# High part of x ahead of the sum in an FFT kernel's three-product mixing, inverse constants on SP's queue, two residues mixed plainly

## The chip, the cores and the metric

The kernel runs on one NeuronCore of a Trainium2 chip. Its engines are PE (TensorE, matmuls), DVE (VectorE), ACT (ScalarE), POOL (GpSimd) and SP (SyncE, which here only issues transfers). The metric is the device time of one execution in microseconds. A change is compared by the median of several runs of the kernel before and after it; smaller is better.

## What is computed

The reference is a chain of three layers on x of 4 x 3072 x 256 float32: a mixing layer in the frequency domain, a gated feed-forward layer and a channel-mix layer. Only the first is touched here.

```python
X = np.fft.rfft(x, axis=1)
Xr, Xi = X.real, X.imag
Yr = Xr @ w_r - Xi @ w_i + b_r
Yi = Xr @ w_i + Xi @ w_r + b_i
Yr = np.sign(Yr) * np.maximum(np.abs(Yr) - 0.01, 0.0)
Yi = np.sign(Yi) * np.maximum(np.abs(Yi) - 0.01, 0.0)
y = np.fft.irfft(Yr + 1j * Yi, n=3072, axis=1)
...                                    # feed-forward: h = y @ w_in; g = h * tanh(softplus(h)); x = g @ w_out
...                                    # channel mix: relu(xk @ w_k)**2 @ w_v, gated by sigmoid(xr @ w_r)
```

## The kernel before

**Two parts.** `part1` does the frequency layer, some 326 us of the span. `part2` does the other two layers; it is put in order by a planner of its own, and the diff doesn't touch it.

**Part 1 in steps.** A transform of 3072 points is split into 24 x 128. DVE does the 24-point butterflies on the batch's tile `a` (the "f1" operations, in the background), and PE does the 128-point transforms as matmuls with constants. The frequencies fall into NT = 12 residues per batch, and with 4 batches there are 48 residues u = 0 to 47. The loop at line 1011 makes one step per u. For a residue, the work is:

- F(u) (`emit_F`): 8 matmuls of `a` with forward constants `fm` into the PSUM tile `xps` (two banks in turn). The result holds the real part xr and the imaginary part xi.
- `post_F(u)`: its evacuation. Matmuls run on rounded "high" parts and on remainders, "low" parts, so `xh` is a copy of `xps` by ACT and `xl` is `xps` minus `xh` by DVE.
- Mixing, in one of two ways, into the PSUM tile `yps` (three banks in turn), which ACT fills with the bias first (`preload`). *Plain*: `emit_M`, 12 matmuls 512 wide, high x high, high x low and low x high. *Three-product* (`gauss(u)` true): G1 (`emit_G1`) multiplies the sum xr + xi by w_r into the first half of `yps`, ACT copies this half into the second (`copy_G`), and G2 (`emit_G2`) adds xr (w_i - w_r) and -xi (w_r + w_i). The sum needs an ACT copy of xr into `xsf`, a DVE addition of xi into `xsf`, and then a high and a low part of its own (the tile named `xs`).
- `post_M(u)`: the soft threshold, two ACT passes into `yb` (from u = 42 on one ACT pass and one of DVE).
- I(u) (`emit_I`): 8 matmuls of `yb` with the inverse constants `im` into `bps`. `post_I(u)` copies it with ACT to `bs`, and SP stores it.

In step u, instructions are emitted in this order: F of the residue ahead, `post_M(u-1)`, `post_I(u-2)`, `post_F` of the residue ahead, G1(u+1) and its copy, M(u) or G2(u), `preload(u+2)`, I(u-1), and the step's transfers. The residue ahead is u + 1 up to LEAD = 7 and u + 2 behind it; step 7 emits both F(8) and F(9). Each engine carries out its own instructions in that order. In steps 35 to 42 `post_I` stands later, behind the weights' work.

**Background work.** DVE also does the butterflies of the next batch, those of the inverse transform ("f3", tile `g`), and the preparation of weights for part 2. The class `Background` decides by a simple clock model where they are put between the steps' own DVE operations: `bg.until(t)` emits background operations until its model clock reaches t, `bg.spend(ready, cost)` charges the clock for the step's own work, and `bg.flush(due)` emits what must not come later. `pe` is the model's clock of PE, with T_F, T_M, T_G1, T_G2 and T_I as durations in ns, and `e` is the model's end of F.

**Queues.** The constants of I(u) come from DRAM, one load of 256 KB per residue, into three slots in turn. Load n may start when the inverse that last used its slot is done. It is emitted at the end of a step, right behind I(u-1), whose slot it takes, and it is needed by I(u+2). The first three go over SP's queue, the others over POOL's:

```python
(nc.gpsimd if n >= len(RING) else nc.sync).dma_start(out=z, in_=isrc[:, t])
```

POOL's queue also carries the loads of x that add to what is in the tile (`end_sum`, steps 6 and 17). SP's queue carries all other loads of x, the stores of `bs`, the loads of weights and the transfers of the inverse transform.

Of the kernel before, what the change touches and what calls it, by code (L numbers as in the profile page):

```python
# [11 lines left out]
F32 = mybir.dt.float32  # L12
F32R = mybir.dt.float32r
I32 = mybir.dt.int32
ACTF = mybir.ActivationFunctionType
ALU = mybir.AluOpType
ADD, SUB, MULT = ALU.add, ALU.subtract, ALU.mult
# [8 lines left out]
NB = 4  # L26
# [6 lines left out]
NT = 12  # L33
# [5 lines left out]
F1_AT = ((4, 4), (0, 0), (0, 0))  # L39
EARLY, REST, LAND = 4, 2, 3  # L40
START = (18600, 20500)
SLACK = (2000, 3200, 600, 1500)
T_F, T_M, T_G1, T_G2, T_I = 1600, 2860, 730, 1690, 1725

SUMS_AT = (11, 12, 23, 24)
# [4 lines left out]
LEAD = 7  # L50
# [131 lines left out]
def tile_fft_mix_moe_channel_mix(  # L182
# [19 lines left out]
    nc = tc.nc  # L202
# [3 lines left out]
    def pool(stack, name, bufs, **kw):  # L206
        return stack.enter_context(tc.tile_pool(name=name, bufs=bufs, reuse_waits="tile", **kw))
# [5 lines left out]
    def tt(o, a, b, op):  # L213
        V.tensor_tensor(out=o, in0=a, in1=b, op=op)  # L214
# [4 lines left out]
    def act(o, i, f, **kw):  # L219
        S.activation(out=o, in_=i, func=f, **kw)  # L220
# [16 lines left out]
    mat = pool(ctx, "mat", 1)  # L237
# [9 lines left out]
    RING = (14, 16, 17)  # L247
# [281 lines left out]
    bg = Background()  # L529
# [162 lines left out]
    def part1():  # L692
        with ExitStack() as es:
# [17 lines left out]
                load_x(As[b], b)  # L711

            xt, xsum, ybt, ybs, xps, yps, bps, lows, flow, xsp, spare = {}, {}, {}, {}, {}, {}, {}, {}, {}, {}, {}
            gauss = lambda u: u > LEAD + 1 and u % NT

            def emit_F(u):
                b, t = u // NT, ORD[u % NT]
                A = As[b]
                ps = psx.tile([128, 2, 256], F32, tag="x", name="xps")
                lr, li = LINES_F[t]  # L720
                line = lambda h, l: A[:, l, h, :]
                if b == 0 and t == 4:
                    lr, li = 20, 21
                if b == 0 and t < 4:
                    line = lambda h, l: G0[:, LINES_G[l - 16], h, :]
                half = lambda z, i: z.rearrange("p (r i f) -> p r i f", r=2, i=2)[:, :, i, :]
                for h in range(2):
                    if t:
                        mm(ps[:, h, :], line(h, lr), fm[t][:, 0, :], True, False)
                        mm(ps[:, h, :], line(h, li), fm[t][:, 1, :], False, True)  # L730
                    else:
                        for i, l in enumerate((lr, li)):
                            mm(half(ps[:, h, :], i), line(h, l), half(fm[0][:, i, :], i), True, True)
                xps[u] = ps
# [14 lines left out]
            def post_F(u):  # L749
                t = u % NT  # L750
                ps = xps.pop(u)
                if u % 3:
                    xh, xl = [xs_p.tile([128, 2, 256], F32R, tag=w, name=w) for w in ("xh", "xl")]
                else:
                    xh, xl = [slot(F32R, w, 2, i) for w, i in (("xh", 12), ("xl", 13))]
                if gauss(u):
                    act(xsf, ps[:, :, 0:128], ACTF.Copy)
                    tt(xsf, ps[:, :, 128:256], xsf, ADD)
                act(xh, ps, ACTF.Copy)
                tt(xl, ps, xh.bitcast(F32), SUB)  # L760
                xt[u] = (xh, xl)
                if gauss(u):
                    z = mat.tile([128, 512], F32R, tag="m%d" % (22 if u % 2 else 15), name="xs").rearrange(
                        "p (s h f) -> p s h f", s=2, h=2)
                    sh, sl = xsum[u] = z[:, 0], z[:, 1]
                    act(sh, xsf, ACTF.Copy)
                    tt(sl, xsf, sh.bitcast(F32), SUB)
                if t == 0:
                    zh, zl = (new_z(w).rearrange("p (h f) -> p h f", h=2) for w in ("zh", "zl"))
                    xt[u] += (zh, zl)  # L770
                    copy_z(u, 0)
                    if u == 0:
                        copy_z(u, 1)

            def copy_z(u, k):
                zz, xx = xt[u][2 + k], xt[u][k]
                S.activation(out=zz, in_=xx.bitcast(F32), func=ACTF.Copy)
                S.activation(out=zz.rearrange("p h (r f) -> p (h r) f", r=2)[:, :, 0:1],
                             in_=zero[:, 0:4].rearrange("p (a o) -> p a o", o=1), func=ACTF.Copy)

            def preload(u):
                ps = yps[u] = psy.tile([128, 512], F32, tag="y", name="yps")
                if gauss(u):
                    act(ps[:, 0:256], bias[:, 0:256], ACTF.Copy)
                    return
                act(ps, bias, ACTF.Copy)
                if u % NT == 0:
                    act(ps[0:1, 256:512], bias[0:1, 0:256], ACTF.Copy)
# [82 lines left out]
            def load_stream(n):  # L871
                _, u, kind = stream[n]
                t = ORD[u % NT]
                z = slot(F32 if kind == "im" else F32R, kind, 2, RING[n % len(RING)])
                (flow if kind == "fmlo" else lows if kind == "imlo" else im)[u] = z
                if kind == "im":
                    (nc.gpsimd if n >= len(RING) else nc.sync).dma_start(out=z, in_=isrc[:, t])
                else:
                    nc.gpsimd.dma_start(out=z, in_=planes[:, kind != "fmlo", t, kind != "imhi"].rearrange("p (r f) -> p r f", r=2))

# [37 lines left out]
            isrc = inv.rearrange("p t (r f) -> p t r f", r=2)  # L918
# [43 lines left out]
            m = split_mix(c1, mraw[0], 0) + split_mix(c1, mraw[1], 1)  # L962
            xsf = c1.tile([128, 2, 128], F32, name="xsf")
# [5 lines left out]
            def gauss_w(h):  # L969
                q = pools["st"].tile([128, 512], F32, tag="q", name="q", bufs=3)  # L970
                hi, lo = wt["gauss", h]
                wr, wi = mraw[h][:, 0, :], mraw[h][:, 1, :]

                def low():
                    act(hi, q, ACTF.Copy)
                    tt(lo, q, hi.bitcast(F32), SUB)
                return [(420.0, lambda: tt(q[:, 0:256], wi, wr, SUB)),
                        (420.0, lambda: stt(q[:, 256:512], wr, -1.0, wi, MULT, SUB)), (700.0, low)]

            def gauss_b():  # L980
                q = pools["st"].tile([128, 512], F32, tag="q", name="q", bufs=3)

                def low():
                    act(brow, q[:, 0:256], ACTF.Copy)
                    act(ones, fm[1][:, 0, 0:128], ACTF.Copy, scale=0.0, bias=1.0 / 64)
                    tt(brow[64:128], q[64:128, 0:256], brow[64:128].bitcast(F32), SUB)
                return [(420.0, lambda: tt(q[:, 0:256], bias[:, 256:512], bias[:, 0:256], SUB)), (420.0, low)]
# [8 lines left out]
            bg.add(priced(rest + first), 4)  # L996
            bg.add(priced(tail[:7]), 5)
            bg.add(priced(tail[7:]), 8)
            bg.add(gauss_w(0) + gauss_w(1) + gauss_b(), LEAD + 2)
            NU = NB * NT  # L1000
            mv[0] = ysrc = None

# [7 lines left out]
            x_at, y_at = {0: bg.clock}, 0.0  # L1010
            for u in range(NU):
                b, t = divmod(u, NT)
# [9 lines left out]
                if u == SUMS_AT[0] - 4:  # L1022
# [10 lines left out]
                                 [(group(g), 2, LOWS_AT - 2 + g, LOWS_AT + g) for g in range(4, 8)] +  # L1033
                                 [(lambda i=i: wout_piece(i), 2, LOWS_AT + 6 + k, LOWS_AT + 8 + k) for k, i in enumerate((0, 4, 1, 5))])
                    emit(wq.load(u))
                ahead = [v for v in ([u + 1] if u < LEAD else [u + 1, u + 2] if u == LEAD else [u + 2]) if v < NU]
                bg.flush(max(ahead, default=u))
                if u == 6:
                    S.activation(out=mu1, in_=mu, func=ACTF.Copy, scale=-1.0, bias=1.0)
                f_end = []  # L1040
# [8 lines left out]
                if u and u - 1 not in TWO_PASS:  # L1049
                    bg.until(y_at + (900 if u - 1 in SPLIT_I else SLACK[0]))  # L1050
                    post_M2(u - 1)
# [21 lines left out]
                behind = []  # L1073
                if u >= SUMS_AT[0] - 3:
                    emit(wq.sca(u, 2))
                    behind = wq.vec(u, 4)
                for v, e in zip(ahead, f_end):
                    bg.until(e + 700 + (0 if u == 0 else SLACK[2] if v % NT == 0 else SLACK[3] if gauss(v) else SLACK[1]) - sum(c for c, e in behind))
                    post_F(v)
                    x_at[v] = bg.spend(e + 700, 602)  # L1080
                    if gauss(v):
                        x_at[v] = bg.spend(e + 1300, 900)
                if u >= SUMS_AT[0] - 3:
                    bg.flush(-1)
                    for c, e in behind:
# [5 lines left out]
                if u + 1 < NU and gauss(u + 1):  # L1091
                    emit_G1(u + 1)
                    copy_G(u + 1)
                    pe = max(pe, x_at[u + 1] + 300) + T_G1
                emit_M(u, None if u else 1)
                if u + 2 < NU:
                    preload(u + 2)
                if (u + 1) % NT == 0 and u + 1 < NU:
                    copy_z(u + 1, 1)
                pe = pe + T_G2 if gauss(u) else max(pe, x_at[u] + 300) + (T_M if u else 900)  # L1100
                y_new = pe + 700
                if u:
                    emit_I(u - 1)
                    pe = max(pe, y_at + 300) + T_I
                y_at = y_new
                if u + NT in SPLIT_F:
                    load_fwd(u + NT)
# [569 lines left out]
```

## Time and profile before

| | us |
|---|---|
| median of 3 runs (1874.37 to 1876.4) | 1875.39 |
| the profiled execution, its own time | 1874.67 |
| its span, first to last instruction | 1872.9 |
| PE busy in the span | 1846.2 (99%) |
| DVE busy | 1413.5 (75%) |
| ACT busy | 1247.7 (67%) |
| POOL busy | 46.0 (2%) |

The span is what the profile shows; the rest of an execution's time lies around it. Times in rows count from the start of the span. A row of the timeline gives the start and the duration of an instruction, or of several merged ones, and in brackets how long its engine stood idle before it and what ended that idle time. Matmuls are pipelined: a row's duration holds the last one's way through the array as well, so the start of one group to the start of the next is the better measure of what a group costs.

### The profile page before, as it was taken

What the parts mean: (1) busy time and instruction counts of PE and PEld (TensorE: products, weight loads), DVE (VectorE), ACT (ScalarE), POOL (GpSimd) and SP (SyncE); (2) the same over time, 40 slices, a digit from 0 to 9 for tenths busy, and PEclk for the clock granted to TensorE, in tenths of its full rate; (3) what the DMA queues carried; (4) which work ended last, traced back from release to release, by engine and by line L of the source; (5) the groups of instructions that cost most, each with busy time, mean ns of one, the idle gap of its engine ahead of it and who ended that gap; (6) DMA issues with size and microseconds to landing.
All of it is one profiled execution on the core that took longest, in us unless ns stands there. A gap on an engine that the chain in (4) does not pass through costs nothing.

```text
span 1872.9 us, 27574 instructions
## 1 busy us (share of the span) xinstructions
PE 1846.2 (99%) x9902; PEld 1600.6 (85%) x9902; DVE 1413.5 (75%) x2537; ACT 1247.7 (67%) x2306; POOL 46.0 (2%) x74
## 2 busy tenths in 40 slices
PE   9899999999999999999999999999999999999999
PEld 7788887888888888888888888888999999999998
DVE  8888867888798879597877768576676666666654
ACT  3566588665667566575766657576877777777775
POOL 1211000000000000000000000000000000000000
PEclk9999999999999999999999999999999999999999
DMA  8849367645646554545546455452422222222211
GB/s 264 230 153 275 113 221 257 190 151 183 195 145 199 164 177 134 179 149 163 185 141 196 145 158 171 138 179 86 158 73 68 68 68 68 68 68 69 68 46 34
DMA packets 183016, 271.57 MB, mean 145 GB/s; under 512 B 16416, under 2 KB 106272, under 8 KB 182624
## 3 DMA queue, kind: packets, MB, share of 16 engines
q1 hardware_dynamic: 173920, 252.77, 42.9%
q0 software_dynamic: 7888, 15.99, 3.5%
q8 instruction: 79, 1.29, 0.3%
q10 hardware_dynamic: 1072, 1.05, 0.2%
q14 instruction: 57, 0.47, 0.1%
HBM read 193.20 MB, written 76.55 MB: 144 GB/s over the span
## 4 chain that ended last, share of the span: by engine, by line
PE 87%; DVE 5%; ACT 3%; DMA 3%; issue 1%; POOL 0%; SPq 0%; DVEq 0%; POOLq 0%; ACTq 0%
PE a L223 28%; PE x L223 16%; PE v L223 14%; PE c L223 10%; PE z L223 5%; PE d L223 5%; PE zps L223 4%; DMA a<-in_x_dram 2%; PE yps L223 2%; PE xps L223 1%; PE bps L223 1%; DVE a L214 1%; DMA im<-in_inv_dram 1%; ACT xh L220 1%; DVE g L214 1%
## 5 line engine op out<-in xcount | busy, mean ns | idle before, releaser
L214 DVE TENSOR_TENSOR l<-k,h 128x512 fp32r<-128x512 f32 x576 | 391.7, 688 | 304.7 <-ACT k L220 150.6
L223 PE MATMUL a<-h,wo 128*128 128x512 f32 x1536 | 520.8, 389 | 0.0
L223 PEld LDWEIGHTS a<-h,wo 128*128 128x128 f32 x1536 | 288.3, 188 | 60.1
L223 PE MATMUL a<-l,wo 128*128 128x512 f32 x768 | 298.8, 389 | 0.0
L223 PE MATMUL v<-wv,h 128*128 128x256 f32 x1536 | 274.4, 278 | 0.0
L223 PEld LDWEIGHTS v<-wv,h 128*128 128x128 f32 x1536 | 244.4, 188 | 13.7
L220 ACT ACTIVATE k<-c 128x512 f32<-128x512 f32 x288 | 172.9, 600 | 108.4 <-PE c L223 96.2
L223 PE MATMUL x<-yc,wr 128*128 128x512 f32 x864 | 243.2, 390 | 0.0
L220 ACT ACTIVATE c<-x 128x512 f32<-128x512 f32 x288 | 169.6, 589 | 89.4 <-PE x L223 75.0
L220 ACT ACTIVATE k<-k 128x512 f32<-128x512 f32 x288 | 178.1, 633 | 65.5 <-DVE k L214 63.3
L223 PE MATMUL v<-wv,l 128*128 128x256 f32 x768 | 213.0, 277 | 0.0
L223 PEld LDWEIGHTS x<-yc,wr 128*128 128x128 f32 x864 | 161.9, 188 | 34.5 <-ACT d L220 0.4
L220 ACT ACTIVATE d<-x 128x512 f32<-128x512 f32 x144 | 84.6, 587 | 145.7 <-PE x L223 144.6
L223 PEld LDWEIGHTS a<-l,wo 128*128 128x128 f32 x768 | 144.2, 188 | 29.9
L223 PE MATMUL c<-yc,wr 128*128 128x512 f32 x576 | 161.8, 389 | 0.0
L223 PEld LDWEIGHTS v<-wv,l 128*128 128x128 f32 x768 | 144.4, 188 | 0.0
L220 ACT ACTIVATE h<-k 128x512 fp32r<-128x512 f32 x192 | 118.6, 629 | 30.2 <-DVE k L217 28.2
L214 DVE TENSOR_TENSOR k<-d,zs 128x512 f32<-128x512 f32 x144 | 98.8, 686 | 42.4 <-PE d L223 42.0
L223 PEld LDWEIGHTS c<-yc,wr 128*128 128x128 f32 x576 | 108.1, 188 | 22.6
L214 DVE TENSOR_TENSOR yc<-src,yc 128x512 fp32r<-128x512 f32 x168 | 112.1, 686 | 14.3 <-ACT yc L220 13.8
L223 PE MATMUL x<-yc,wk 128*128 128x512 f32 x432 | 122.5, 392 | 0.0
L214 DVE TENSOR_TENSOR g<-g 128x128 f32<-128x128 f32 (+3 forms) x264 | 110.7, 442 | 0.9
(128 smaller groups left out, 2907.7 us busy)
## 6 DMA issues: line engine op xcount, KB each, us to landing
wr<-h_dr SPq DMA_DIRECT2D x288, 256.0 KB, 2.8
b_dr<-bs SPq DMA_DIRECT2D x48, 256.0 KB, 3.5
src<-y_dr SPq DMA_DIRECT2D x24, 512.0 KB, 4.1
wr<-h_dr SPq DMA_DIRECT2D x96, 128.0 KB, 2.1
xk_dr<-tm SPq DMA_DIRECT2D x48, 256.0 KB, 3.1
xr_dr<-tm SPq DMA_DIRECT2D x48, 256.0 KB, 3.2
xr<-xr_dr SPq DMA_DIRECT2D x24, 512.0 KB, 3.8
src<-xk_dr SPq DMA_DIRECT2D x24, 512.0 KB, 4.2
```

The costliest lines, as they stand in the source:

```text
L214: V.tensor_tensor(out=o, in0=a, in1=b, op=op)
L220: S.activation(out=o, in_=i, func=f, **kw)
L223: T.matmul(out=o, lhsT=l, rhs=r, start=start, stop=stop, **kw)
```

## The change

In three-product residues ACT now makes `xh` directly behind its copy of xr, and DVE's addition for the sum comes behind that. The sum's high and low part move out of `post_F` into a function `post_sum`, which is called at the end of the step, behind M(u) and `preload(u+2)`. The model's times for background work around them change with it. In step 7, F(9) and its evacuation move from behind F(8) to the end of the step. Residues 46 and 47 are mixed plainly. All inverse constants go over SP's queue. The weights of the three-product form get a later due time.

```diff
-SLACK = (2000, 3200, 600, 1500)
+SLACK = (2000, 3200, 600)
...
-            gauss = lambda u: u > LEAD + 1 and u % NT
+            gauss = lambda u: LEAD + 1 < u < NB * NT - 2 and u % NT
...
                 if gauss(u):
                     act(xsf, ps[:, :, 0:128], ACTF.Copy)
+                act(xh, ps, ACTF.Copy)
+                if gauss(u):
                     tt(xsf, ps[:, :, 128:256], xsf, ADD)
-                act(xh, ps, ACTF.Copy)
                 tt(xl, ps, xh.bitcast(F32), SUB)
                 xt[u] = (xh, xl)
-                if gauss(u):
-                    z = mat.tile([128, 512], F32R, tag="m%d" % (22 if u % 2 else 15), name="xs").rearrange(
-                        "p (s h f) -> p s h f", s=2, h=2)
-                    sh, sl = xsum[u] = z[:, 0], z[:, 1]
-                    act(sh, xsf, ACTF.Copy)
-                    tt(sl, xsf, sh.bitcast(F32), SUB)
...
+            def post_sum(u):
+                z = mat.tile([128, 512], F32R, tag="m%d" % (22 if u % 2 else 15), name="xs").rearrange(
+                    "p (s h f) -> p s h f", s=2, h=2)
+                sh, sl = xsum[u] = z[:, 0], z[:, 1]
+                act(sh, xsf, ACTF.Copy)
+                tt(sl, xsf, sh.bitcast(F32), SUB)
...
-                    (nc.gpsimd if n >= len(RING) else nc.sync).dma_start(out=z, in_=isrc[:, t])
+                    nc.sync.dma_start(out=z, in_=isrc[:, t])
...
-            bg.add(gauss_w(0) + gauss_w(1) + gauss_b(), LEAD + 2)
+            bg.add(gauss_w(0) + gauss_w(1) + gauss_b(), LEAD + 4)
...
-                ahead = [v for v in ([u + 1] if u < LEAD else [u + 1, u + 2] if u == LEAD else [u + 2]) if v < NU]
+                ahead = [v for v in [u + 1 if u <= LEAD else u + 2] if v < NU]
...
-                    bg.until(e + 700 + (0 if u == 0 else SLACK[2] if v % NT == 0 else SLACK[3] if gauss(v) else SLACK[1]) - sum(c for c, e in behind))
+                    bg.until(e + 1500 if gauss(v) else e + 700 + (0 if u == 0 else SLACK[2] if v % NT == 0 else SLACK[1]) - sum(c for c, e in behind))
                     post_F(v)
-                    x_at[v] = bg.spend(e + 700, 602)
-                    if gauss(v):
-                        x_at[v] = bg.spend(e + 1300, 900)
+                    x_at[v] = bg.spend(e + (1100 if gauss(v) else 700), 980 if gauss(v) else 602)
...
                 if u + 2 < NU:
                     preload(u + 2)
+                for v in ahead:
+                    if gauss(v):
+                        bg.until(f_end[0] + 2700)
+                        post_sum(v)
+                        x_at[v] = bg.spend(f_end[0] + 2700, 400)
...
                 if u:
                     emit_I(u - 1)
                     pe = max(pe, y_at + 300) + T_I
+                if u == LEAD:
+                    bg.flush(u + 2)
+                    emit_F(u + 2)
+                    pe += T_F
+                    bg.until(pe + 700)
+                    post_F(u + 2)
+                    post_sum(u + 2)
+                    x_at[u + 2] = bg.spend(pe + 1100, 1380)
```

## Rows read from the trace of the kernel before

**Rows 1.** Waits of PE, 15 to 330 us: total, times, longest

```profile
PE yps L223 <- ACT yps L220: 9.3, 13, 1.8
PE bps L223 <- DMA im<-in_inv_dram: 5.5, 2, 2.9
PE bps L223 <- DVE yb L217: 2.1, 3, 1.0
PE xps L223 <- DVE xl L214: 2.1, 2, 1.2
```

**Rows 2.** Timeline of PE: the inverse matmuls of steps 21 to 25

```profile
164.36 1.89 PE L223 MATMUL bps<-im,yb 128*128 128x256 f32 x8
169.25 1.89 PE L223 MATMUL bps<-im,yb 128*128 128x256 f32 x8
174.26 1.89 PE L223 MATMUL bps<-im,yb 128*128 128x256 f32 x8
181.30 1.89 PE L223 MATMUL bps<-im,yb 128*128 128x256 f32 x8
187.03 1.89 PE L223 MATMUL bps<-im,yb 128*128 128x256 f32 x8
```

**Rows 3.** Windows: busy PE, PEld, DVE, ACT, POOL, clock, DMA share, GB/s

```profile
103.56:181.30 77.74, 71.86 (x427) 64.41 (x426) 65.61 (x127) 46.12 (x105) 13.72 (x18) 0.98 0.82 234
181.30:257.88 76.58, 71.93 (x428) 64.64 (x427) 64.03 (x126) 44.69 (x104) 6.45 (x12) 0.98 0.40 122
257.88:311.52 53.64, 52.35 (x317) 47.44 (x316) 38.30 (x80) 48.44 (x106) 4.84 (x9) 1.00 0.88 297
```

**Rows 4.** Timeline of all engines around the longest wait of G1

```profile
239.91 0.42 DVE L214 TENSOR_TENSOR xsf<-xps,xsf 128x256 f32<-128x256 f32 x1
240.35 0.60 ACT L220 ACTIVATE xh<-xps 128x512 fp32r<-128x512 f32 x1 [3.75 <-DVE xsf L214]
...
241.46 0.37 ACT L220 ACTIVATE yps<-bias 128x256 f32<-128x256 f32 x1
...
241.88 0.50 PE L223 MATMUL yps<-wmh,xs 128*128 128x256 f32 x2 [1.84 <-ACT yps L220]
```

**Rows 5.** Waits of all engines, 15 to 330 us

```profile
ACT xh L220 <- DVE xsf L214: 70.6, 36, 5.3
...
DVE xl L214 <- ACT xh L220: 24.7, 38, 0.7
```

**Rows 6.** Timeline of POOL: three loads in one row

```profile
149.33 2.21 POOL L877 DMA_DIRECT2D im<-in_inv_dram  x3
```

**Rows 7.** Timeline of PE: inverses behind late constants, and the one between

```profile
84.90 2.57 PE L223 MATMUL bps<-im,yb 128*128 128x256 f32 x8 [2.62 <-DMA im<-in_inv_dram]
...
91.50 1.89 PE L223 MATMUL bps<-im,yb 128*128 128x256 f32 x8
...
156.88 2.85 PE L223 MATMUL bps<-im,yb 128*128 128x256 f32 x8 [2.88 <-DMA im<-in_inv_dram]
```

**Rows 8.** Window behind the first late constant, columns as in rows 3

```profile
85.00:89.00 4.00, 4.00 (x17) 3.60 (x18) 3.34 (x9) 3.10 (x7) 0.54 (x1) 0.64 1.09 376
```

**Rows 9.** DMA issues: size, median us to landing

```profile
im<-in_inv_dram POOLq DMA_DIRECT2D x45, 256.0 KB, 3.3
...
a<-in_x_dram SPq DMA_DIRECT2D x13, 512.0 KB, 9.0
```

**Rows 10.** Timeline of DVE and PE in step 8

```profile
70.36 0.68 DVE L214 TENSOR_TENSOR xl<-xps,xh 128x512 fp32r<-128x512 f32 x1
...
71.10 1.99 PE L223 MATMUL xps<-fm,a 128*128 128x256 f32 x8 [0.90 <-DVE xl L214]
```

**Rows 11.** Timeline of PE: two inverses with a plain step between

```profile
40.33 1.89 PE L223 MATMUL bps<-im,yb 128*128 128x256 f32 x8
...
46.52 1.89 PE L223 MATMUL bps<-im,yb 128*128 128x256 f32 x8
```

**Rows 12.** Tile `wg`, its making: ns least, median, most; first and last start

```profile
L214 DVE TENSOR_TENSOR wg<-q,wg x2: 692/692/693, 48.2 to 51.3; 128x512 fp32r<-128x512 f32 x2
```

## The prediction

> **What bounds the kernel.** I read the page's busy shares first: PE is busy for 99% of the span, so only its idle time and its own work can move the end. The waits of PE come next [rows 1]. All that matter lie before 326 us, in the first part (FFT, mixing, inverse); the channel mix after it runs without gaps, and the diff does not touch it. Four kinds stand there: 13 waits of G1 matmuls for an ACT copy into `yps` (9.3 us), two for an inverse constant (5.5), three for DVE's `yb` (2.1), two for DVE's `xl` (2.1).
>
> The rows of the inverse matmuls show what a step costs without a wait, start to start [rows 2]: 5.73 us for a full three-product step, 4.89 and 5.01 for the two around a batch's turn, 7.04 for the plain step of t = 0. Twelve steps without a wait are 4.89 + 5.01 + 7.04 + 9 x 5.73 = 68.5 us. The windows [rows 3] show 77.74 for steps 12 to 23 and 76.58 for steps 24 to 35; the nine steps behind them take 53.64 where 51.6 would do. Excess: 9.2 + 8.1 + 2.0 = 19.3 us, of which 4.6 is the second wait for a constant (below). The G1 waits thus cost 14.7, more than the 9.3 of the waits view: the weight loads in front cannot be hidden either, and after the longest one the clock is lower.
>
> **Why G1 waits.** The timeline of one stall [rows 4] is to be read backwards: G1 starts at 241.88, when ACT's preload of `yps` ends; the preload stands in ACT's line behind the copy of G1's result, the high part of the sum and `xh`; `xh` had stood 3.75 us waiting for DVE's add, which came late behind background butterflies. The waits of all engines [rows 5] show this in all 36 three-product residues: ACT stands 70.6 us at `xh` for the add, then DVE stands for `xh` (24.7 us in 38 times, 0.65 each) before `xl`. So DVE loses 0.65 us per residue, 7 us per batch, on top of 65.6 us of work [rows 3], and ACT is shut while DVE is late.
>
> **The sum.** All terms are against the profiled run, 1874.67 us around a span of 1872.9; the median of the runs is 0.7 above it.
>
> *T1, constants on SP's queue.* The load stands on POOL's queue behind the accumulating x loads, which wait for each other; three loads then go at once [rows 6]. PE idles 2.62 us and 2.88 us, and the step behind each is long: 84.90 to 91.50 is 6.60 instead of 4.89, 156.88 to 164.36 is 7.48 instead of 5.73 [rows 2, 7]. There the granted clock is 0.64 in a stretch, between the levels of 1.2 and 2.4 GHz [rows 8]. Together 2.62 + 1.71 + 2.88 + 1.75 = 9.0 us. On SP the load waits for I(u-1), as before. Queued behind it is the store of that same residue, which waits for a copy of I(u-1)'s result, so for something later still; weight and x loads behind it lose at most the rest of a step, and are issued steps ahead of their use. From the end of I(u-1) to I(u+2) there are 3 x 5.73 - 1.89 = 15.3 us. A landing takes 3.3 us from POOL and x loads on SP 9.0 [rows 9], so 6.3 us remain at the worse end. Gain 9.0; bounds 0 (as late as now; later only if SP ran further behind than POOL does behind its x loads) and 9.0.
>
> The Trainium skill ("DMA: Bandwidth & Descriptors", Queues, rings and completion order) says that each DMA engine consumes one queue's descriptors in ring order and takes turns between queues. By that rule the constant, now in the ring of the x loads, cannot pass them, where POOL's ring took turns. By it the landing is the slower one and the gain is the same while the margin lasts; no row here shows a constant behind an x load, and this is a reason for rival C.
>
> *T2, xh ahead of the add, the sum's parts at the end.* ACT no longer waits for DVE at `xh`; only the high part of the sum does, and now behind the copy of G1 and the preload. DVE can run add and `xl` back to back if `xh` is ready. The emission model also changes: a three-product post had been charged 602 + 900 ns and takes, with its wait, 0.42 + 0.65 + 0.68 + about 0.4 = 2.1 us [rows 4, 5, 10], so DVE slid back some 0.6 us a step until G1 stopped it. It is now charged 980 + 400 and takes 1.5 at most. A batch then needs 65.6 us of DVE in 68.5: PE is again the slower one, by a little. In the nine steps of the third row of the windows ACT is the tight one (48.4 of 51.6). Bounds: 0 (the wait only changes sides; below that only by D) and 14.7. With engines at 94 to 96% I do not expect all of it; I take three quarters, 11.0.
>
> The Trainium skill ("PSUM — Partial Sum Buffer", PSUM bank collisions raise a hardware error) states that two engines must not access one bank at once, even to read, so they have to be ordered. By it the add, which reads `xps` like `xh`, now waits for `xh`: the wait is turned round. By the row alone the add would be free. By the rule DVE may still stand up to one `xh` (0.60 us), though not where it comes late, which is where G1 stalls; this is rival B.
>
> *T3, step 7.* F(9) moves from behind F(8) to the end of step 7. F(10) takes the bank of F(8), and that is free only when DVE has written `xl` of residue 8: 70.36 + 0.68, and F(10) starts at 71.10 [rows 10]. DVE is full there, so this stays, and the 2.1 us of waits [rows 1] with it. But add(9), which ran right behind that `xl`, now comes after up to 2.4 us of background (two pieces of 1.13), and G1(9) follows F(10) at once: the sum's high part is ready at about 70.96 + 2.27 + 0.42 + 0.41 = 74.1, against 71.1 + 1.6 = 72.7 (the 1.99 of F's row less its overlap with what follows). Loss 1.4, and if the idle before F(10) grows to that of the constants, 1.7 of slower clock and perhaps 1.0 more: bounds -1.4 and -4.1; I take -2.0, nearer the row without a slow clock. The later due time of the three-product weights costs nothing: the background reached them by itself, the second at 51.3 us [rows 12], long before G2(9), which runs just ahead of the inverse at 84.90; without that cover two pieces of 0.69 us and what leads to them would stand ahead of G2(9).
>
> *T4, residues 46 and 47 plain.* A plain step takes 46.52 - 40.33 = 6.19 [rows 11] against 5.73: 0.46 each, +0.92 of PE work. It falls where PE waits anyway: the three waits for `yb` are the last three inverses (2.1 us) [rows 1], and G1(47) is among the waits for `yps`, 0.7 us each on average. ACT loses two narrow copies and a high part per residue there, DVE an add and a low part. With 0.7 us of waiting left, the gain is 2.1 + 0.7 - 0.7 - 0.92 = 1.2. Bounds -0.9 (no wait shrinks) and +1.9.
>
> Sum: 9.0 + 11.0 - 2.0 + 1.2 = 19.2 us. On the median 1875.4 - 19.2 = **1856**. Everything at its good end: 9.0 + 14.7 - 1.4 + 1.9 = 24.2, or 1851; T2 at half: 1860; T3 at its bad end as well: 1862. 1851 to 1862 is the likeliest case's own range.
>
> **Rivals.** *B, the wait changes sides* (0.13). DVE stands for ACT at the add instead of at `xl`, so DVE's loss of 0.65 stays and only ACT is freed; it takes a quarter of T2, 3.7 us: 9.0 + 3.7 - 2.0 + 1.2 = 11.9, 1864. For it: add and `xl` both need `xh` of the same bank. Against it: `xh` now needs only one ACT copy behind F, and a late DVE finds it done.
>
> *C, the constants stay late* (0.07). SP's line holds x loads, stores and weight loads in order; if it runs 12 us behind I(u-1) in steps 6 and 17, T1 is 0: 10.2 gained, 1865. Against it: the margin above.
>
> *D, slower* (0.07). The sum's high part stands behind the copy of G1's result, and its low part stands in DVE's line behind it. If G1 is late, ACT waits at the copy, DVE waits for copy, preload and high part (three narrow passes of about 0.37 [rows 4], 1.1) with all its butterflies behind, so the next add and the next G1 are late: a loop. It must cost more than the 0.65 per residue that goes. At 0.5 more in 31 residues it costs 15.5, less T1, T3 and T4 (8.2): 7.3 slower, 1883. It decides from 8.2 / 31 = 0.26 a residue on. Against it: G1 takes 5.73 - 5.01 = 0.72 us [rows 2] and on time ends a microsecond after F, so the high part is ready before the 2.7 us at which the low part is emitted.
>
> *E, DVE was the bound all along* (0.05). Background work refills whatever is freed and early constants only move the wait to the next G1: T1 and T2 shrink to 4 us together, T3 and T4 take 0.8: 1872, within what a measurement can tell from no change (0.2%, 3.7 us). For it: work and its 0.65s fill 73 of the 77.7 us of steps 12 to 23 [rows 3]. Against it: 65.6 is under 68.5, and the third window, with 38.3 us of DVE in 53.6, has room for what is put off.
>
> **How the numbers follow.** Forecast 0.68, B 0.13, C 0.07, D 0.07, E 0.05. Faster 0.68 + 0.13 + 0.07 = 0.88; same 0.05; slower 0.07. The range 1849 to 1867 holds nearly all of the forecast, B's and C's centres, and leaves D and E out.
>
> **What would show it.** Right: no PE wait for an inverse constant, no granted clock below 0.9 near 85 and 157; no ACT wait of `xh` for DVE's add; twelve steps in 69 to 71 us instead of 77; the last inverse 17 to 21 us earlier; a G1 wait left in step 8. Wrong: PE waiting for `xs` in most steps, DVE idle at the sum's low part (D) or at the add (B), constants issued on SP long behind I(u-1) (C).

## The result, and the profile after

| | median of the runs | profiled run | span |
|---|---|---|---|
| before | 1874.9 us (1872.0 to 1876.4) | 1874.7 | 1872.9 |
| after | 1852.4 us (1852.3 to 1853.4) | 1852.6 | 1850.6 |

After over before is 0.9883 (95% interval 0.9866 to 0.9900): 22.4 us faster, where 19.2 had been forecast. The spans differ by 22.3.

The waits of PE in the first part, 15 to 330 us, of the changed kernel; this is all of that answer, and stands against [rows 1] (columns: us in total, times, longest):

```profile
PE xps L223 <- DVE g L214: 2.3, 1, 2.3
PE xps L223 <- DVE xl L214: 2.2, 1, 2.2
PE bps L223 <- DMA im<-in_inv_dram: 1.8, 1, 1.8
PE yps L223 <- ACT xh L220: 0.7, 1, 0.7
```

The 13 waits of G1 for an ACT copy into `yps` are gone, and so are the three for `yb`. Of the two waits for a constant one of 1.8 us is left, but it is a new one, in step 24 (below). The two waits for `xl` have become one of about the same sum. The 2.3 us for `g` stand ahead of the very first F (last section).

The waits of all engines in the same stretch answer to [rows 5]:

```profile
ACT xsf L220 <- PE xps L223: 25.2, 21, 5.3
DVE xsf L214 <- ACT xh L220: 18.6, 17, 3.1
ACT xs L220 <- DVE xsf L214: 13.7, 13, 3.9
...
DVE xl L214 <- ACT xh L220: 4.1, 4, 2.1
```

ACT's 70.6 us at `xh` for DVE's add no longer appear. ACT now mostly waits for PE, which is what a helper of the bound engine should wait for. DVE's 38 waits ahead of `xl` are 4; in their place stand 17 ahead of the add (`xsf`), 18.6 us. So the wait did turn round, but only in about half the residues.

The windows of the same three stretches, inverse to inverse, columns as in [rows 3] (us; busy PE, PEld, DVE, ACT, POOL; clock; DMA share; GB/s):

```profile
101.70:172.34 70.64, 68.81 (x427) 63.72 (x426) 65.95 (x130) 48.74 (x107) 7.20 (x6) 1.00 0.81 227
172.34:240.89 68.55, 68.55 (x425) 63.74 (x426) 61.50 (x123) 45.40 (x101) 0.00 (x0) 1.00 0.52 169
240.89:291.71 50.82, 50.82 (x311) 47.05 (x310) 37.62 (x79) 48.85 (x107) 0.00 (x0) 1.00 0.95 317
```

Steps 24 to 35 take 68.55 us, the floor of 68.5 worked out from [rows 2]: PE is busy all the time at full clock. Steps 12 to 23 take 2.1 us more than that, 1.83 of it the wait for the constant. PE has no idle time in the third stretch either, though ACT is busy for 96% of it; it is 0.7 us below the floor there, since a plain residue 46 has no G1 in step 45. DVE's busy time is what it was (65.95 us, where it was 65.61).

An ordinary step of the changed kernel in the timeline of all engines (start, us, engine, line, instruction, idle before it and what ended that); it answers to [rows 4]:

```profile
111.08 0.38 ACT L220 ACTIVATE xsf<-xps 128x256 f32<-128x256 f32 x1 [1.13 <-PE xps L223]
111.36 0.59 ACT L220 ACTIVATE xh<-xps 128x512 fp32r<-128x512 f32 x1
111.84 0.39 ACT L220 ACTIVATE yps<-yps 128x256 f32<-128x256 f32 x1
112.14 0.39 ACT L220 ACTIVATE yps<-bias 128x256 f32<-128x256 f32 x1
...
113.75 0.42 DVE L214 TENSOR_TENSOR xsf<-xps,xsf 128x256 f32<-128x256 f32 x1
114.09 0.68 DVE L214 TENSOR_TENSOR xl<-xps,xh 128x512 fp32r<-128x512 f32 x1
114.20 0.42 ACT L220 ACTIVATE xs<-xsf 128x256 fp32r<-128x256 f32 x1 [1.68 <-DVE xsf L214]
```

DVE comes to the add 1.8 us after `xh` has ended, but ACT has done the copy of G1's result and the preload in the meantime (112.5) and waits only afterwards, where nothing of PE's hangs on it yet. In [rows 4] the same lateness of DVE stood ahead of both. Add and `xl` follow each other without a gap.

**Where the 22.3 us come from**, stretch by stretch of the two traces, start of an inverse to start of an inverse (I5 is residue 5's):

| stretch | before | after | difference |
|---|---|---|---|
| start to I5 | 58.89 | 59.84 | +0.95 |
| I5 to I9 | 32.61 | 29.81 | -2.80 |
| I9 to I11 | 12.06 | 12.05 | 0 |
| steps 12 to 23 | 77.74 | 70.64 | -7.10 |
| steps 24 to 35 | 76.58 | 68.55 | -8.03 |
| steps 36 to 44 | 53.64 | 50.82 | -2.82 |
| I44 to the start of `part2` | 14.27 | 12.22 | -2.05 |
| `part2` | | | -0.45 |

`part2` is what the prediction calls the channel mix. The first row is not the change's: it arises around the first F, and the profiles of the experiments below have either value (last section). So differences of a microsecond between two kernels are to be read stretch by stretch.

### The profile page after: what moved, and what is told of

It is laid out like the page before. It is cut to its first block, busy times and chain, and to the rows that moved or that the text cites. A ratio compares the mean times of both kernels' runs of the same rounds, so it can differ in the third digit from the quotient of the medians.

```text
span 1850.6 us, 27511 instructions
## 1 busy us (share of the span) xinstructions
PE 1838.1 (99%) x9888; PEld 1599.2 (86%) x9888; DVE 1409.3 (76%) x2533; ACT 1248.9 (67%) x2300; POOL 19.3 (1%) x29
## 4 chain that ended last, share of the span: by engine, by line
PE 96%; DVE 3%; DMA 1%; ACT 0%; issue 0%; SPq 0%; DVEq 0%
PE a L223 28%; PE x L223 16%; PE v L223 14%; PE c L223 11%; PE z L223 5%; PE d L223 5%; PE yps L223 5%; PE bps L223 4%; PE zps L223 4%; PE xps L223 3%; DVE a L214 1%; DVE a L217 1%; DMA a<-in_x_dram 0%; DMA im<-in_inv_dram 0%; DVE xl L214 0%; DVE g L214 0%
## 5 line engine op out<-in xcount | busy, mean ns | idle before, releaser
L220 ACT ACTIVATE k<-k 128x512 f32<-128x512 f32 x288 | 178.1, 633 | 65.8 <-DVE k L214 63.6
```

## The experiments

Each experiment's ratio is to the kernel before, run beside it on the same chip (medians 1874.0 to 1875.3). "Undone" means the changed kernel with one part taken back, "alone" the kernel before with one part put in.

**The queue undone, and alone.** The first takes the constants back to POOL in the changed kernel, the second puts them on SP in the kernel before (the same line the other way round).

```diff
-                    nc.sync.dma_start(out=z, in_=isrc[:, t])
+                    (nc.gpsimd if n >= len(RING) else nc.sync).dma_start(out=z, in_=isrc[:, t])
```

> The changed kernel with the inverse constants back on POOL's queue, nothing else. Theory (T1 stands by itself): the two waits for a constant in steps 9 and 20 come back with their slow clock, the one of 1.8 us in step 24 goes; some 5 to 8 us slower than the changed kernel, 1857.5 to 1860. Rival C or E (the queue does not matter, DVE or another wait takes its place): within 2 us of the changed kernel's 1852.4.

Measured 1858.6 us, 0.9911 (0.9894 to 0.9927): 6.2 more than the changed kernel, so the queue matters there, as expected. Not all of it is the queue's: in the profile steps 12 to 23 take 75.96, 5.3 more, while I5 to I9 takes 31.76, 1.95 more, because the granted clock stays low longer behind the idle time of step 7 (0.62 from F(10) to I(7), 0.76 in the changed kernel), and the start is 1.1 shorter. Its only wait of PE for a constant:

```profile
PE bps L223 <- DMA im<-in_inv_dram: 5.5, 1, 5.5
```

It is the second of the two. The first does not come back: POOL issues that constant hardly earlier (at 75.55, before at 75.84), but PE reaches the inverse later because of step 7, at 85.64 where it had stood waiting from 82.3.

> The kernel before with all inverse constants on SP's queue, nothing else. Theory: both waits for a constant go, but the G1 waits stay, and part of what is won is lost to the next G1, since DVE stays late: 5 to 9 us faster than before, 1866 to 1870. Rival E (DVE was the bound): under 3 us.

Measured 1871.4 us, 0.9975 (0.9965 to 0.9984): -3.4, under what was expected, and nearly what rival E would have. Both waits for constants are gone, and PE's waits of G1 have grown from the 9.3 us in 13 times of [rows 1]:

```profile
PE yps L223 <- ACT yps L220: 14.7, 16, 1.9
```

What PE no longer loses at the constant it loses at the next G1, because DVE is behind in any case. In the kernel before, then, T1 was worth 3.4 and not 9.0.

**The order alone, the model's times alone, and both main parts.** In the kernel before, `xh` is put ahead of the add and nothing else changes:

```diff
                     act(xsf, ps[:, :, 0:128], ACTF.Copy)
+                act(xh, ps, ACTF.Copy)
+                if gauss(u):
                     tt(xsf, ps[:, :, 128:256], xsf, ADD)
-                act(xh, ps, ACTF.Copy)
```

> The kernel before with xh ahead of the add, the sum's parts still in the evacuation and the model's times as they were. Theory (DVE's 0.65 us per residue and ACT's wait at xh were what held G1): most of the 14.7 us of G1 waits go, 8 to 13 us faster, the two waits for a constant stay: 1862 to 1867. Rival B (the wait only changes sides): ACT is still shut by the sum's high part, which stands ahead of the copy and the preload, 0 to 4 us faster. Rival F (it is the model's charge, not the order, that ends the waits): 0 to 4 us as well, and then the run with the model's times alone shows the gain.

Measured 1867.6 us, 0.9959 (0.9946 to 0.9973): -7.2, between the theory's range and the rivals'. PE's waits say why:

```profile
PE bps L223 <- DMA im<-in_inv_dram: 6.4, 1, 6.4
...
PE yps L223 <- ACT yps L220: 1.2, 2, 0.6
```

```profile
85.88 3.42 PE L223 MATMUL bps<-im,yb 128*128 128x256 f32 x8 [2.77 <-ACT yb L220]
```

The G1 waits are nearly gone (1.2 us), and steps 24 to 35 take 68.49 us, the floor. But PE, no longer held up at G1, reaches I(19) earlier and waits 6.4 us there for the same late constant, where 2.9 had been lost [rows 7]; steps 12 to 23 still take 77.3. The other late constant is still late too: it is the wait of the row above, which the view puts down to ACT's `yb`, but I(8)'s `yb` was done at 79.1, and its constant landed at 85.7. It is the mirror image of the queue alone: two waits stand in one path, and whichever is removed, the other takes up what is won.

The emission model's due time and charge, alone in the kernel before:

```diff
-                    bg.until(e + 700 + (0 if u == 0 else SLACK[2] if v % NT == 0 else SLACK[3] if gauss(v) else SLACK[1]) - sum(c for c, e in behind))
+                    bg.until(e + 1500 if gauss(v) else e + 700 + (0 if u == 0 else SLACK[2] if v % NT == 0 else SLACK[1]) - sum(c for c, e in behind))
                     post_F(v)
-                    x_at[v] = bg.spend(e + 700, 602)
-                    if gauss(v):
-                        x_at[v] = bg.spend(e + 1300, 900)
+                    x_at[v] = bg.spend(e + (1100 if gauss(v) else 700), 1380 if gauss(v) else 602)
```

> The kernel before with the changed kernel's times for background work around a three-product evacuation (until 1500 ns behind F, charge 1380), and no change in order. Theory: the emission allows about as much background work per step as before, DVE still loses 0.65 us a residue, so the G1 waits stay: within 3 us of before. Rival F (the times alone end the waits): 8 us faster or more.

Measured 1874.3 us, 0.9994 (0.9985 to 1.0004), with G1 waits of 8.8 us in 12: no change. The larger charge is not a cause by itself.

Order and queue together, in the kernel before, without the step-end sum, the move of F(9) and the plain residues:

> The kernel before with two parts of the change alone: xh ahead of the add, and all constants on SP's queue; the sum's parts, the model's times, F(9) and the last residues as before. Theory (the two parts each take away what absorbed the other's gain, so together they give more than the 7.2 and 3.4 us apart): 1874.9 - 4.3 - 9.2 + 2.5 - 8.1 - 0.6 = 1855, between 1852 and 1858. Rival (the sum's parts at the step's end are needed for the rest): 1861 to 1865, the sum of the two alone.

Measured 1855.0 us, 0.9886 (0.9870 to 0.9903): -20, as expected. The parts alone give 3.4 and 7.2, together 20; all the rest of the change adds 2.6. Behind the order the queue is worth 12.6, behind the queue the order 16.4. What the rest does is seen late in the first part. PE's timeline of three inverses there, and the three waits for `yb` of [rows 1], which this kernel still has:

```profile
268.64 1.89 PE L223 MATMUL bps<-im,yb 128*128 128x256 f32 x8
...
275.23 1.89 PE L223 MATMUL bps<-im,yb 128*128 128x256 f32 x8
...
281.84 1.89 PE L223 MATMUL bps<-im,yb 128*128 128x256 f32 x8
```

```profile
PE bps L223 <- DVE yb L217: 2.1, 3, 1.0
```

These steps take 6.6 us, as in the kernel before (286.64, 293.28, 299.92), and 5.73 in the changed one. Of its other parts only the sum's parts at the step's end, with their due times, reach this stretch. They are needed here, but not enough: with them and the old order (next experiment) three of these steps take 6.6 us again.

**The add first again.** The changed kernel with add and `xh` in the old order, all else kept:

```diff
                     act(xsf, ps[:, :, 0:128], ACTF.Copy)
-                act(xh, ps, ACTF.Copy)
-                if gauss(u):
                     tt(xsf, ps[:, :, 128:256], xsf, ADD)
+                act(xh, ps, ACTF.Copy)
```

> The changed kernel with only the order of the evacuation undone: the add ahead of xh again, the sum's parts still at the step's end. Theory: ACT waits at xh for DVE again and DVE for xh, 0.65 us a residue, so G1 waits come back in part; the sum's parts at the end keep some of the gain: 3 to 10 us slower than 1852.4. If the place of the sum's parts is what matters: under 2 us.

Measured 1868.8 us, 0.9970 (0.9958 to 0.9982): 16.3 more than the changed kernel, and more than expected. In the waits of all engines the wait of [rows 5] is back at its old size, and PE's waits show G1 held up, now by the two parts of the sum:

```profile
ACT xh L220 <- DVE xsf L214: 73.4, 34, 4.6
...
PE yps L223 <- ACT xs L220: 6.5, 11, 1.4
PE yps L223 <- DVE xs L214: 5.0, 7, 1.1
```

So it is the order of these two instructions that carries T2. Putting the sum's parts at the step's end without it makes them late.

**How much DVE can bear.** Two kernels give DVE more work in each three-product residue of the changed kernel: `xl` is computed a second time (0.6 us), or its first half is (0.33 us).

```diff
                 tt(xl, ps, xh.bitcast(F32), SUB)
+                if gauss(u):
+                    tt(xl, ps, xh.bitcast(F32), SUB)
```

> The changed kernel in which DVE writes the low part xl of a three-product residue twice with the same values: 0.6 us more of DVE per residue, uncharged in the model, about what the old order lost. Theory (DVE's time is the margin: 66 us in 68.6): a batch then needs 72.6, G1 waits come back, 3 to 5 us in each of batches 1 and 2, 6 to 10 us in all. Rival (ACT shut by DVE was the whole cause, DVE's own time is not near the bound): under 2 us.

> The changed kernel in which DVE writes half of the low part of a three-product residue a second time with the same values: 0.33 us more of DVE per residue. Theory (DVE's time is the margin, and the whole 0.6 us cost 9.9 us): a batch needs 66 + 3.6 = 69.6 us against 68.5, so 0.5 to 1.5 us in each of batches 1 and 2 and little elsewhere: 1 to 4 us slower than 1852.4. Rival (any addition makes the next one late in a loop, D): 8 us or more.

Measured 1862.4 us, 0.9935 (0.9920 to 0.9950), 9.9 more than the changed kernel; and 1855.2 us, 0.9892 (0.9878 to 0.9907), 2.7 more. Both totals as expected, and the second is far under rival D's loop. But the second does not lie where it was expected, in batches 1 and 2 alike: steps 12 to 23 take 2.0 us more than in the changed kernel, 24 to 35 take 0.1 and 36 to 44 take 1.2 more. The windows of steps 12 to 23 and 24 to 35 with `xl` twice, and then of steps 24 to 35 with half of it twice:

```profile
102.50:174.40 71.90, 70.20 (x428) 64.14 (x427) 70.69 (x136) 44.33 (x101) 7.20 (x6) 1.00 0.79 226
174.40:247.88 73.48, 70.53 (x428) 64.18 (x427) 70.53 (x138) 45.64 (x107) 0.00 (x0) 1.00 0.47 152
```

```profile
173.55:242.18 68.63, 68.63 (x426) 63.81 (x427) 65.84 (x135) 44.20 (x102) 0.00 (x0) 1.00 0.52 169
```

With `xl` twice, DVE's 70.5 us are more than the 68.5 that PE needs, so DVE sets the step, and PE waits 14 times for the sum's low part (6.3 us). At 65.8 us, in the last window, PE sets it and has no idle time.

**F(9) back behind F(8).** The changed kernel with step 7 emitted as before:

```diff
-                ahead = [v for v in [u + 1 if u <= LEAD else u + 2] if v < NU]
+                ahead = [v for v in ([u + 1] if u < LEAD else [u + 1, u + 2] if u == LEAD else [u + 2]) if v < NU]
...
-                if u == LEAD:
-                    bg.flush(u + 2)
-                    emit_F(u + 2)
...
```

> The changed kernel with F(9) back behind F(8) in step 7, the sum's parts of residue 9 at the end of that step. Theory (T3 is a loss of its own): F(10) is still held by the low part of residue 8, but G1(9) no longer comes late and the clock stays up: 1 to 3 us faster than 1852.4, 1849.5 to 1851.5. Rival: DVE is full there, and what is won is lost again before step 12: within 1 us.

Measured 1851.0 us, 0.9874 (0.9860 to 0.9889): 1.4 less than the changed kernel, inside the range that was expected, but not for its reason alone. In the profiles I5 to I9 takes 28.12 instead of 29.81, 1.7 less; all of that is lost again around the constant of step 24, which now makes PE wait 2.3 us (2.0 us more in steps 12 to 35), and what is left between the two spans is the start, 1.2 us earlier. The timeline of PE around F(10) and the window from there to I(7), first in the changed kernel, then in this one:

```profile
71.85 2.91 PE L223 MATMUL xps<-fm,a 128*128 128x256 f32 x8 [2.21 <-DVE xl L214]
74.90 0.80 PE L223 MATMUL yps<-wmh,xs 128*128 128x256 f32 x2
```

```profile
71.85:79.03 7.18, 7.05 (x27) 5.52 (x27) 5.23 (x9) 3.69 (x9) 3.50 (x3) 0.76 1.10 189
```

```profile
63.50 0.70 PE L223 MATMUL xps<-fm,a 128*128 128x256 f32 x2 [1.23 <-DVE xl L214]
...
70.86 2.00 PE L223 MATMUL xps<-fm,a 128*128 128x256 f32 x8 [0.88 <-DVE xl L214]
72.51 0.59 PE L223 MATMUL yps<-wmh,xs 128*128 128x256 f32 x2
```

```profile
70.86:76.16 5.30, 5.30 (x27) 4.60 (x28) 5.30 (x8) 3.67 (x9) 2.20 (x2) 1.00 1.14 262
```

With F(9) behind F(8), PE stands twice for `xl`, 1.23 and 0.88 us, at full clock; with F(9) at the end of the step it stands once, 2.21 us, and the granted clock is 0.76 over what follows. The sum of the idle time is the same.

**The three-product form to the end.** The changed kernel with residues 46 and 47 mixed by three products again:

```diff
-            gauss = lambda u: LEAD + 1 < u < NB * NT - 2 and u % NT
+            gauss = lambda u: u > LEAD + 1 and u % NT
```

> The changed kernel with residues 46 and 47 in three products again. Theory (T4): ACT's passes come later in the last three steps, the waits for yb come back, and the 0.9 us of PE work saved do not pay for them: 1 to 3 us slower than 1852.4. Rival: with the G1 waits gone the waits for yb are gone too, then it is 0.9 us faster.

Measured 1852.0 us, 0.9879 (0.9862 to 0.9895): 0.5 less than the changed kernel, within the measurement's noise; the expectation was missed. From I43 to the start of `part2` it takes 17.32 us, the changed kernel 17.22. PE waits 0.8 us for `yb`, once, where it waited 2.1 [rows 1].

**The best of it.** F(9) back behind F(8), and constants on SP only where POOL's x loads would hold them up:

```diff
-                    nc.sync.dma_start(out=z, in_=isrc[:, t])
+                    (nc.sync if n < len(RING) or u in (8, 9, 10, 19, 20, 21) else nc.gpsimd).dma_start(out=z, in_=isrc[:, t])
```

> The changed kernel with F(9) back behind F(8), and with constants on SP's queue only where POOL's is full of accumulating loads of x (residues 8 to 10 and 19 to 21), on POOL's elsewhere. Theory (the wait left in step 24 comes from SP's line of inverse-transform stores and x loads): that wait of 2.3 us and 1.8 us of slow clock behind it go, 1851.0 - 4.1 = 1847, between 1845.5 and 1848.5. Rival (the constant is late there on any queue, since the x loads fill the DMA engines): 1850 to 1852.

Measured 1848.2 us, 0.9853 (0.9838 to 0.9867): 4.3 less than the changed kernel, and every one of its runs is under every one of that kernel's. It is in the range expected, and PE waits for no constant. But in its profile the stretch of I23 to I25 is still 2.3 us longer than it need be: DVE now waits 4.7 us for a load of x there, so the sum's low part is late. The first row is POOL's issue of the constant of I(23), the second PE's wait in step 24:

```profile
152.62 0.57 POOL L879 DMA_DIRECT2D im<-in_inv_dram  x1 [5.14 <-DMA y_dr<-g]
```

```profile
172.86 0.51 PE L223 MATMUL yps<-wmh,xs 128*128 128x256 f32 x2 [1.40 <-DVE xs L214]
```

> The run before this one with residues 46 and 47 in three products as well. Theory (plain mixing there costs in PE work what it saves in waits): within 1 us of the run before it. Rival (T4 as predicted): 1 to 3 us slower.

Measured 1848.6 us, 0.9854 (0.9839 to 0.9868): the same. The plain residues do nothing here either.

## Why the prediction was right, point by point

The predicted time, 1856 in 1849 to 1867, held, by the likeliest case's steps: the late constants, the order and step 7. The sizes of its terms were off, and partly off against one another: T1 (1.9 too high) and T4 (1.2 too high) against T2 (3.4 too low) and 2.8 at the end of the first part, which came from elsewhere than T4 had it. That the sum came out within 3.2 us is partly luck.

**T1, 9.0 predicted, 7.1 in the trace.** The windows that hold the two late constants lost 4.33 and 4.63 us of waiting and slow clock, the whole 9.0, but 1.83 came back as a new wait in step 24. The first of the two is not the queue's alone: with the queue undone it does not come back, because step 7's delay (T3) gives that constant the time it lacked. SP's timeline of the changed kernel shows where (lines: L400 stores, L362 x loads, L879 constants):

```profile
159.49 2.92 SPq L400 DMA_DIRECT2D y_dr<-g  x4
162.46 2.11 SPq L362 DMA_DIRECT2D a<-in_x_dram  x4
164.66 0.59 SPq L879 DMA_DIRECT2D im<-in_inv_dram  x1
```

and PE's timeline, inverse I(20), which makes the buffer free, and I(23), which uses it:

```profile
153.24 1.89 PE L223 MATMUL bps<-im,yb 128*128 128x256 f32 x8
...
172.34 1.97 PE L223 MATMUL bps<-im,yb 128*128 128x256 f32 x8 [1.83 <-DMA im<-in_inv_dram]
```

The load could go at 155.1, goes at 164.66 behind the stores and four x loads, and has landed 7.5 us later; the median landing of the 48 constants on SP is 3.4. That is rival C's mechanism, at one place of 48. The step that failed is the margin of 15.3 less 9.0: it set only the x loads' own landing against the margin, and put the line in front of the load at nothing, while here it was 9.5 us, and 9.5 + 7.5 is more than 15.3. The best version has this load on POOL's queue, with 38 others: it goes 0.3 us behind the end of I(20), lands 3.9 us later, and the wait is gone. The Trainium skill ("DMA: Bandwidth & Descriptors", Queues, rings and completion order) has the ring order by which a constant cannot pass x loads in front of it. The 7.5 us fit that but do not show it: in the best version the next three constants on POOL's queue, in another ring than SP's x loads, took 6.1 to 7.3 us to land.

**T2, 11.0 predicted, 14.4 in the trace** (4.3 + 8.0 + 2.1 of the three windows, of 14.7). The step was right in its mechanism: order undone costs 16.3. It was mis-sized: a quarter was held back for engines at 94 to 96% of a step, and PE lost nothing with DVE that full. What decides is DVE's work against the 68.5 us that PE needs: with 61.5 us of it (the changed kernel) and 65.8 us (half of `xl` twice) in steps 24 to 35 PE had no idle time, with 70.5 us (`xl` twice) the same steps took 5 us longer. The 2.1 of the third window, where ACT is the tight one, need both parts of the step: the order without the sum's parts at the step's end takes 53.36 there (order and queue together), the sum's parts at the end without the order 53.61 (the add first again), both together 50.82. The part of the step on the emission model's charge fell: changed alone it does nothing, and with the new order and the old charge steps 24 to 35 already take 68.5.

**T3, -2.0 predicted, -1.7 measured** by F(9) put back. The step named a G1 late by 1.4 us behind two background pieces, and the trace has it: from F(10)'s start to G1's it takes 3.05 us instead of 1.65, with the two pieces ahead of the add and G1's first weight load waiting for the sum's high part:

```profile
71.71 2.35 DVE L214 TENSOR_TENSOR a<-a 128x1024 f32<-128x1024 f32 x2
73.98 0.41 DVE L214 TENSOR_TENSOR xsf<-xps,xsf 128x256 f32<-128x256 f32 x1
...
74.89 0.50 PEld L223 LDWEIGHTS yps<-wmh,xs 128*128 128x128 f32 x2 [0.85 <-ACT xs L220]
```

F(10) itself runs at the lower clock meanwhile (2.91 us in its row instead of 2.00) and ends just before, so this trace alone does not tell the two causes apart. The kernel with `xl` twice does: there F(10) takes 1.99 us and G1 still starts 3.05 us behind its start, waiting for the sum:

```profile
70.90 1.99 PE L223 MATMUL xps<-fm,a 128*128 128x256 f32 x8 [2.41 <-DVE xl L214]
73.95 0.50 PE L223 MATMUL yps<-wmh,xs 128*128 128x256 f32 x2 [1.05 <-ACT xs L220]
```

A further 0.5 behind G1 is the slower clock after the merged idle of 2.21 us, which had stood as the worse end, and 0.2 is won ahead of F(10). The 1.7 is no fixed price: with the queue undone and with `xl` twice the stretch takes 31.8 us, 3.6 more than with F(9) put back.

**T4, +1.2 predicted, 0 measured.** The end did get shorter, by 2.05 us, and with the 0.7 of step 45 by 2.8; but it does so with three products too. The waits for `yb` were still there with order and queue alone (2.1 us in 3), are 0.8 in one with the whole change but the plain residues, and none with the sum's parts at the end in the old order (the add first again), where I43 to the start of `part2` takes the changed kernel's 17.22 us. So it is the sum's parts at the step's end that took them away. The step put down to itself a gain that another part of the change gives.

**B** was right that the wait turns round (DVE ahead of the add, 18.6 us) and wrong on its price. The Trainium skill ("PSUM — Partial Sum Buffer", PSUM bank collisions raise a hardware error) has the reason why it must: two engines may not read one bank at once. The trace agrees: 17 of the 34 adds start only when `xh` has ended. But DVE stands there only where it comes early, and PE shows no wait for it.

**D** fell: its sign, PE waiting for `xs` in most steps, is not among the waits of PE, and 0.33 us more per residue, over its point of 0.26, cost 2.7 us and started no loop.

**E** fell for the whole change and was nearly right for its parts: alone, the queue gave 3.4 of its 9.0, since DVE's lateness took the rest. What settles it is both parts in the kernel before, -20 us. The sum of the prediction added T1 and T2 as if each were worth its own waits; that holds for both together, and for neither alone.

Left open: the 0.45 us of `part2`, which the diff does not touch, were not looked into.

## What to carry to other kernels

Two waits on one path take up each other's gain: trying the changes one at a time would have shown 3.4 and 7.2 us and hidden that both together are worth 20, so fixes for waits that follow each other should be tried together before one is dropped. Where two engines read one result, let the engine go first whose queue holds work that the bound engine needs next; the other's lateness then costs nothing as long as its work fits into the step (here 65.8 us in 68.5, and no longer 70.5). Before a load is moved to another queue, count all that will stand in front of it there at its own moment, not the landing of the queue's typical transfer alone.

## What the runs showed of the hardware that was not expected

**Short idle times and the clock.** An idle of TensorE of 1.84 us was followed by a granted clock of 0.76 over the next 7 us in the kernel before (242 to 249 us), one of 2.21 us by 0.76 over the next 7 (the window from F(10) above), and one of 2.31 us, at the constant of step 24 with F(9) put back, by the 0.77 below; one of 1.83 us, at the same place in the changed kernel, by 1.00. The window of the kernel before, and those of the step behind each of the last two, first the changed kernel's, then that with F(9) put back:

```profile
242.00:249.00 7.00, 7.00 (x34) 6.45 (x35) 5.51 (x10) 6.03 (x13) 0.54 (x1) 0.76 0.36 112
```

```profile
172.40:178.10 5.70, 5.70 (x35) 5.29 (x36) 5.25 (x9) 2.90 (x7) 0.00 (x0) 1.00 1.03 418
```

```profile
169.80:177.20 7.40, 7.40 (x35) 6.48 (x36) 5.28 (x9) 2.90 (x7) 0.00 (x0) 0.77 0.95 379
```

The same 35 matmuls take 1.7 us more in a stretch that is partly at 1.2 and partly at 2.4 GHz. At this place half a microsecond more of idle time (2.31 after 1.83) cost 2.2. The length of the idle time does not decide alone: 1.83 and 1.84 us had different clocks behind them, and the same idle of 2.4 us ahead of F(10) left a step of 13.0 us from I(6) to I(7) in the kernel with three products to the end, and one of 15.0 with the queue undone, where G1 stood 0.51 us more and the clock was 0.62.

**The start.** In the profile of the changed kernel the granted clock is 0.70 from 16.3 to 22.0 us, behind an idle of 2.27 us ahead of the first F; before it is 1.00 behind an idle of 0.85. The first inverse starts at 28.91 and 27.96. In the experiments' profiles it starts at 27.7 to 27.9 in seven, behind idles of 0.64 to 1.68 us, and at 28.9 to 29.5 in the other five, behind idles of 2.04 to 2.64, and kernels that differ only in the last residues stand in both groups: a spread of over 1 us that no part of the change was seen to set.
